# The first load of an attention-and-MLP kernel, q and k of one tile, cut into two transfers by heads

## The chip, the cores and the metric

The kernel runs on 1 core of one Trainium2 chip. The metric is device microseconds of one execution, as the median of several runs. The execution that the profiler recorded is one more run; its trace is what the rows below come from.

## The reference

Three stages follow one another. First, attention in chunks of 64 positions (4 batches, 8 heads, 576 positions, head size 64):

```
scores = scale * np.matmul(q_c, k_c.transpose(0, 1, 2, 4, 3))
scores = scores - np.max(scores, axis=-1, keepdims=True)
attn = np.exp(scores)
attn = attn / (np.sum(attn, axis=-1, keepdims=True) + 1e-09)
out = np.matmul(attn, v_c)
```

Its output, as 2304 tokens of 512 numbers, goes through an MLP with a SiLU (`h = x @ w_in`, `g = h * sigmoid(h)`, `g @ w_out`, 2048 wide) and then through a gated MLP (`(x @ w_a) * (x @ w_b) @ w_out`, 1536 wide).

## The kernel before

The 2304 tokens are 18 tiles of 128. The attention of tiles 0 to 3 comes first, all by itself; that of the other tiles is worked in between the matrix products of the first MLP. All of the order is written out by hand. A list of loads sets the order in which SP, which issues nearly all DMAs of this stage, issues them:

```
"s t 0, s t 1, s t 2, s w, s t 3, s v 1, s v 0, s w, s v 3, s w, s v 2, s w, s w"
```

Here `t i` is q and k of tile i together (512 KB, [128 partitions x 2 x 512] floats), `v i` is v of tile i (256 KB), and `w` one weight block of the first MLP (512 KB, raw 64-bit words). A second list, `beginning`, sets the order of everything else. Its first words are:

```
"busy 7 at, S 0 at mm, M 0 act, busy 2 acc2, E 0, S 1 sA sB, busy 1 acc2, N1 0, M 1, "
"S 2 acc0 acc1, E 1, busy 5 acc2, M 2 act, mg, N1 1, R 0, N2 0, busy 3 acc2, S 3 at mm, "
```

- `busy n` (line 757) are n matmuls on a tile of zeros, whose results nobody reads. Seven of them go into the bank `ps_at` ahead of `S 0`, which writes the same bank.
- `S i` (`att_scores`, line 295) are the 16 score products of tile i. The outer loop runs over the four head pairs `hp`, and each has four products: two chunks, and two heads of the pair (on partitions 0 to 63 and 64 to 127). Those of tile 0 go to the banks `ps_at` and `ps_mm`. In the trace every product has two records, so that `S 0` has 32.
- `M i` (line 311, and 313 or 316) takes the maxima on VectorE, `E i` (lines 332, 328) the exponentials on ScalarE, `T`, `P`, `V` (lines 369, 373, 394) transpose the probabilities, copy them back and multiply by v. `fa 0` (line 434) is the first product of the MLP.

Every DMA has its own completion count, out of eight that are used in turn (DMAHW0 to DMAHW7), so the ninth DMA of the program waits until the first has landed. `load_qk` (line 275) issues the transfer for tiles 0 to 3; on tiles 4 and later it takes the other branch.

Of the kernel before, what the change touches and what calls it, by code (L numbers as in the profile page):

```python
# [28 lines left out]
def chunk_attention_silu_mlp_gated_mlp(  # L29
# [35 lines left out]
    DM = out_t.shape[0]  # L65
# [29 lines left out]
    def width(b):  # L95
        return blocks[b][1] * P
# [162 lines left out]
    shared = {}  # L259

    def att_tile(where, name, i=0):
        if where == "att":
            return late["att"].tile([P, DM], F32, tag="at", name=name)
        key, n = (i, "qkvs".index(name)) if name in "qkvs" else (("pt", i // 4), i % 4)
        if key not in shared:
            shared[key] = slot("start", F32).rearrange("p (j n) -> p j n", j=4)
        return shared[key][:, n]

    def load_qk(i, where, eng=nc.gpsimd):
        qk[i] = [att_tile(where, nm, i) for nm in "qk"]  # L270
        if where == "att":
            for j, a in enumerate(qk[i]):
                eng.dma_start(out=a, in_=qkt[i][:, j])
        else:
            eng.dma_start(out=shared[i][:, :2], in_=qkt[i])

    def load_v(i, where, eng=nc.gpsimd):
        vs[i] = att_tile(where, "v", i)
# [455 lines left out]
    with tc.manual_schedule():  # L734
# [30 lines left out]
        n = width(SIDE)  # L765
# [9 lines left out]
        for line in loads.split(", "):  # L775
            by, what, *i = line.split()
            if what == "w":
                fetch(*next_a())
            elif what == "v":
                queues[by].dma_start(out=vs[int(i[0])], in_=v[int(i[0])])  # L780
            else:
                load_qk(int(i[0]), W, queues[by])
        load_qk(4, A, nc.sync)
        load_qk(5, A, nc.sync)

        SIDE_FROM = 6
# [898 lines left out]
```

## Time and profile before

| | us |
|---|---|
| median of 3 runs (lowest, highest) | 828.69 (828.15, 830.61) |
| profiled execution: its time | 829.36 |
| profiled execution: its span in the trace | 827.6 |
| PE busy, share of the span | 822.7, 99% |
| ACT busy, share of the span | 460.5, 56% |
| attention of tiles 0 to 3, until the first product of the MLP starts on PE | 0 to 19.77 |

The span is what the trace shows of the execution; 1.76 us of its time lie around it. PE is TensorE, PEld its weight loads, DVE VectorE, ACT ScalarE, POOL GpSimd, SP SyncE; SPq is the issuing of DMAs on SP. A busy PE also counts `busy` matmuls that compute nothing.

### The profile page before, as it was taken

To read this page: it belongs to the slowest core of one execution; us is meant where nothing else is said; L and a number is where in the kernel's file an instruction comes from. 1 tells how busy PE (TensorE), PEld (TensorE's weight loads), DVE (VectorE), ACT (ScalarE), POOL (GpSimd) and SP (SyncE) were. 2 spreads that over 40 slices of the span, in tenths; PEclk is the share of its full clock that TensorE was granted. 3 is DMA by queue.
4 is the path that set the end of the run, shared out by engine and by line. 5 is a ranking of instruction groups with operands and counts; after the bars stand their busy time and mean duration, and the time that the engine had idled before them with its cause. 6 is when DMAs were issued, how large, how long until landed. Compare 5 with 4: busy or idle time off the path is not lost.

```text
span 827.6 us, 14001 instructions
## 1 busy us (share of the span) xinstructions
PE 822.7 (99%) x5428; PEld 754.7 (91%) x5428; DVE 553.9 (67%) x1005; ACT 460.5 (56%) x868; POOL 50.7 (6%) x91
## 2 busy tenths in 40 slices
PE   9999999999999999999999999999999999999998
PEld 8889989888888888888889999999999999999998
DVE  6897576644667788788967995882545593454563
ACT  7997687765677755555744553453333363333252
POOL 1010010031021021100011100000000000000000
PEclk9999999999999999999999999999999999999999
DMA  9786698961375685720189769978677878767741
GB/s 354 260 277 191 196 277 277 271 201 53 108 262 170 221 319 227 288 97 27 65 298 401 293 279 367 331 286 287 246 247 264 326 276 304 267 238 251 282 181 58
DMA packets 52674, 199.10 MB, mean 241 GB/s; under 512 B 5632, under 2 KB 17536, under 8 KB 43136
## 3 DMA queue, kind: packets, MB, share of 16 engines
q1 hardware_dynamic: 43232, 162.78, 55.5%
q0 software_dynamic: 9088, 35.13, 12.1%
q8 instruction: 43, 0.70, 0.3%
q10 hardware_dynamic: 288, 0.30, 0.1%
q14 instruction: 23, 0.19, 0.1%
HBM read 147.32 MB, written 50.86 MB: 239 GB/s over the span
## 4 chain that ended last, share of the span: by engine, by line
PE 98%; DMA 2%; ACT 0%; issue 0%; SPq 0%
PE ps_acc L1006 26%; PE ps_acc L483 11%; PE ps_mm L434 8%; PE ps_sA L1006 8%; PE ps_mm L1006 8%; PE ps_sB L1006 7%; PE ps_at L1006 7%; PE ps_acc L434 5%; PE ps_at L434 4%; PE ps_sA L434 4%; PE ps_sB L434 2%; PE ps_sA L483 1%; PE ps_sB L483 1%; DMA ring<-wg 1%; PE ps_at L295 1%; PE ps_at L394 1%
## 5 line engine op out<-in xcount | busy, mean ns | idle before, releaser
L1006 PE MATMUL ps_acc<-xo,ring 128*128 128x384 f32 x902 | 171.9, 334 | 0.0
L1006 PEld LDWEIGHTS ps_acc<-xo,ring 128*128 128x128 f32 x902 | 157.7, 188 | 0.4 <-DVE gq L1081 0.3
L483 PE MATMUL ps_acc<-ghi,wA 128*128 128x512 f32 x256 | 81.1, 398 | 0.0
L1006 PE MATMUL ps_acc<-u,ring 128*128 128x384 f32 x322 | 61.3, 334 | 0.0
L1454 ACT ACTIVATE u<-gq 128x384 fp32r<-128x384 f32 x84 | 40.6, 516 | 30.9 <-DVE gq L1081 28.5
L1006 PEld LDWEIGHTS ps_acc<-u,ring 128*128 128x128 f32 x322 | 56.3, 188 | 0.0
L434 PE MATMUL ps_mm<-xhi,wA 128*128 128x512 f32 (+1 forms) x208 | 54.7, 386 | 0.0
L483 PEld LDWEIGHTS ps_acc<-ghi,wA 128*128 128x128 f32 x256 | 46.1, 188 | 9.4 <-ACT ghi L465 0.2
L1455 DVE TENSOR_TENSOR u<-gq,u 128x384 fp32r<-128x384 f32 x84 | 44.4, 552 | 15.2 <-ACT u L1454 15.0
L483 PE MATMUL ps_acc<-glo,wA 128*128 128x512 f32 x128 | 50.1, 392 | 0.0
L189 ACT ACTIVATE raws<-raws 128x512 f32<-128x512 f32 x62 | 41.7, 673 | 8.2 <-DVE raws L176 8.0
L463 DVE TENSOR_TENSOR glo<-g,ghi 128x512 fp32r<-128x512 f32 (+1 forms) x48 | 28.5, 600 | 25.1 <-ACT ghi L465 24.9
L1015 ACT ACTIVATE gq<-ps_acc 128x384 f32<-128x384 f32 x31 | 15.3, 492 | 52.9 <-PE ps_acc L1006 48.8
L1006 PE MATMUL ps_sA<-xo,ring 128*128 128x384 f32 x220 | 44.4, 334 | 0.0
L1006 PE MATMUL ps_mm<-xo,ring 128*128 128x384 f32 x214 | 43.2, 334 | 0.0
L206 DVE SCALAR_TENSOR_TENSOR w<-raws 128x512 uint32<-128x512 uint32 x42 | 29.0, 691 | 21.1 <-ACT raws L189 13.9
L434 PEld LDWEIGHTS ps_mm<-xhi,wA 128*128 128x128 f32 x208 | 37.0, 188 | 6.6
L1006 PE MATMUL ps_sB<-xo,ring 128*128 128x384 f32 x208 | 42.3, 335 | 0.0
L187 ACT ACTIVATE raws<-raws 128x512 int32<-128x512 uint8 x62 | 42.1, 679 | 0.0
L1006 PE MATMUL ps_at<-xo,ring 128*128 128x384 f32 x202 | 41.1, 335 | 0.3 <-DMA ring<-wg 0.3
L1006 PEld LDWEIGHTS ps_sA<-xo,ring 128*128 128x128 f32 x220 | 38.7, 188 | 0.0
L1006 PEld LDWEIGHTS ps_mm<-xo,ring 128*128 128x128 f32 x214 | 37.7, 188 | 0.0
(270 smaller groups left out, 1734.6 us busy)
## 6 DMA issues: line engine op xcount, KB each, us to landing
ring<-w SPq DMA_DIRECT2D x30, 1024.0 KB, 6.9
ring<-wg SPq DMA_DIRECT2D x28, 1024.0 KB, 7.3
ring<-wg SPq DMA_DIRECT2D x28, 768.0 KB, 4.6
wg<-ring SPq DMA_DIRECT2D x8, 1024.0 KB, 4.2
raws<-w_out SPq DMA_DIRECT2D x14, 512.0 KB, 5.2
raws<-w_in SPq DMA_DIRECT2D x12, 512.0 KB, 5.2
raws<-w_a SPq DMA_DIRECT2D x12, 512.0 KB, 4.7
raws<-w_b SPq DMA_DIRECT2D x12, 512.0 KB, 4.2
```

What stands on the lines that cost most here:

```text
L187: nc.scalar.activation(low.bitcast(I32), top, AF.Copy, scale=2.0**-5, bias=-31 / 64)
L189: nc.scalar.activation(high, high, AF.Prelu, scale=2.0**-112, alpha=-(2.0**32))
L206: nc.vector.scalar_tensor_tensor(out=out.bitcast(U32), in0=high[:, n], scalar=3, in1=low[:, n], op0=ALU.logical_shift_left, op1=ALU.bitwis ...
L295: nc.tensor.matmul(soft[i][0][j][n, hp, :], lhsT=q[r, hp, n], rhs=k[r, hp, n], start=True, stop=True,)
L394: nc.tensor.matmul(ps[half[part], hp, n], lhsT=va[half[r], a, hp, :], rhs=prob[i][half[r], hp, half[a]], start=True, stop=True,)
L434: nc.tensor.matmul(ps[:, n], lhsT=a[:, kk * P:(kk + 1) * P], rhs=b[:, kk, n], start=(j == 0 and kk == 0 and not part), stop=(j == 2 and kk ...
L463: nc.vector.tensor_tensor(out=glo, in0=g, in1=ghi.bitcast(F32), op=ALU.subtract)
L483: nc.tensor.matmul(acc_t[b][j], lhsT=a[:, j * P:(j + 1) * P], rhs=g, start=(m == 0 and i == 0 and (b != SIDE or j % 2 == 0)), stop=(m == M ...
L1006: nc.tensor.matmul(ps, lhsT=a, rhs=b, start=first and i == 0, stop=last and i == 2, skip_group_check=True,)
L1015: nc.scalar.activation(dst, ps, AF.Copy)
L1454: nc.scalar.activation(hi, src, AF.Copy)
L1455: nc.vector.tensor_tensor(out=lo, in0=src, in1=hi.bitcast(F32), op=ALU.subtract)
```

## The change

`load_qk` issues tile 0 as two transfers of 256 KB. The first holds columns 0 to 255 of q and of k (head pairs 0 and 1), the second columns 256 to 511 (head pairs 2 and 3). Tiles 1 to 3 keep their one transfer.

```
         else:
-            eng.dma_start(out=shared[i][:, :2], in_=qkt[i])
+            parts = 2 if i == 0 else 1
+            for n in range(parts):
+                c = slice(n * DM // parts, (n + 1) * DM // parts)
+                eng.dma_start(out=shared[i][:, :2, c], in_=qkt[i][:, :, c])
```

Whole, a partition's row of q and k is 4 KB in one piece; a half is two pieces of 1 KB each. The code below the edit moves down by three lines (295 becomes 298).

On SP, at the start of the program, before (`start` is the tile that holds q, k and v; `first` is the place of the raw weights; the brackets tell which DMA's completion an issue waits for):

```order
L275 DMA start<-qkt 128x1024 x3
L155 DMA first<-w_in 128x512
L275 DMA start<-qkt 128x1024
L780 DMA start<-v 128x512 x2
L155 DMA first<-w_in 128x512
L780 DMA start<-v 128x512 [waits DMAHW0_49]
L155 DMA first<-w_out 128x512 [waits DMAHW1_49]
```

On SP, the same place in the changed kernel:

```order
L278 DMA start<-qkt 128x2x256 x2
L278 DMA start<-qkt 128x1024 x2
L155 DMA first<-w_in 128x512
L278 DMA start<-qkt 128x1024
L783 DMA start<-v 128x512 x2
L155 DMA first<-w_in 128x512 [waits DMAHW0_49]
L783 DMA start<-v 128x512 [waits DMAHW1_49]
L155 DMA first<-w_out 128x512 [waits DMAHW2_49]
```

There is one DMA more, and every later one stands one place further down. The second weight block is now the ninth DMA and waits for the first half of tile 0; v of tile 3 waits for the second half where it waited for the whole; from there on each DMA waits for the same transfer as before, under the next number.

On PE, at the start of the program, before (the seven `busy` matmuls and the score products of tile 0, one row each):

```order
L757 MATMUL ps_at<-start 128x128 x6
L295 MATMUL ps_at<-start 64x64 [waits DMAHW0_49,PE_49]
L295 MATMUL ps_mm<-start 64x64
L295 MATMUL ps_at<-start 64x64
L295 MATMUL ps_mm<-start 64x64
L295 MATMUL ps_at<-start 64x64
L295 MATMUL ps_mm<-start 64x64
L295 MATMUL ps_at<-start 64x64
L295 MATMUL ps_mm<-start 64x64
L295 MATMUL ps_at<-start 64x64
L295 MATMUL ps_mm<-start 64x64
```

On PE, the same place in the changed kernel:

```order
L760 MATMUL ps_at<-start 128x128 x6
L298 MATMUL ps_at<-start 64x64 [waits DMAHW0_49,PE_49]
L298 MATMUL ps_mm<-start 64x64
L298 MATMUL ps_at<-start 64x64
L298 MATMUL ps_mm<-start 64x64
L298 MATMUL ps_at<-start 64x64
L298 MATMUL ps_mm<-start 64x64
L298 MATMUL ps_at<-start 64x64
L298 MATMUL ps_mm<-start 64x64
L298 MATMUL ps_at<-start 64x64 [waits DMAHW1_49]
L298 MATMUL ps_mm<-start 64x64
```

No product has moved. The first still waits for the first transfer and for PE's own `busy` matmuls; the ninth of the sixteen has a wait of its own, for the second transfer. On VectorE, ScalarE and GpSimd the order is the same in both kernels.

## Rows read from the trace of the kernel before

**Rows 1.** The page: span, and shares of the chain that ended last
```profile
span 827.6 us, 14001 instructions
...
PE 98%; DMA 2%; ACT 0%; issue 0%; SPq 0%
```

**Rows 2.** Windows; columns: stretch, length, busy time by engine, PEclk, DMA share, GB/s
```profile
0.00:4.63 4.63, 3.36 (x15) 3.10 (x15) 0.22 (x2) 1.49 (x2) 0.69 (x6) 1.00 0.61 192
4.63:19.77 15.14, 15.06 (x311) 13.28 (x311) 12.94 (x32) 12.74 (x47) 2.65 (x6) 1.00 1.03 402
```

**Rows 3.** The chain in order of time, start of the program: start, length, what
```profile
0.72 3.77 DMA start<-qkt
4.49 0.14 issue
4.63 0.34 PE ps_at L295
```

**Rows 4.** Timeline of PE: start, length, engine, line, tiles, count, [idle before]
```profile
1.07 3.36 PE L757 MATMUL ps_at<-start 128*128 128x128 f32 x14 [1.07 <-DVE start L751]
4.63 0.34 PE L295 MATMUL ps_at<-start 64*64 64x64 f32 x1 [0.20 <-DMA start<-qkt]
...
5.08 0.31 PE L295 MATMUL ps_at<-start 64*64 64x64 f32 x1
...
5.44 0.31 PE L295 MATMUL ps_mm<-start 64*64 64x64 f32 x1
5.68 1.22 PE L757 MATMUL ps_acc<-start 128*128 128x128 f32 x4
6.83 0.29 PE L295 MATMUL ps_sA<-start 64*64 64x64 f32 x1
...
8.52 2.37 PE L757 MATMUL ps_acc<-start 128*128 128x128 f32 x16
...
11.30 0.22 PE L295 MATMUL ps_mm<-start 64*64 64x64 f32 x1
...
14.40 1.15 PE L394 MATMUL ps_sA<-start 64*64 64x64 f32 x32
```

**Rows 5.** Who waited for whom, 0 to 70 us: total, times, longest
```profile
PEld ps_at L295 <- PE ps_at L757: 0.5, 1, 0.5
...
PE ps_at L295 <- DMA start<-qkt: 0.2, 1, 0.2
```

**Rows 6.** DMA traffic in the windows 3 to 4 and 412 to 414.5 us
```profile
DMA packets 113, 0.41 MB, mean 410 GB/s; under 512 B 13, under 2 KB 13, under 8 KB 113
...
DMA packets 924, 0.86 MB, mean 343 GB/s; under 512 B 51, under 2 KB 924, under 8 KB 924
```

**Rows 7.** Issues on SP, ns min/median/max; last line: landing of the yr loads, us
```profile
L275 SPq DMA_DIRECT2D start<-qkt x4: 388/422/477, 0.7 to 2.6; - x4
...
L162 SPq DMA_DIRECT2D wo<-w x8: 372/428/508, 20.7 to 59.5; - x8
...
L663 SPq DMA_DIRECT2D yr<-y x6: 545/602/608, 409.7 to 413.0; - x6
...
DMA to landing us min/median/max: 3.8/4.0/4.6
```

**Rows 8.** Timeline of SP: DMA issues that waited for tiles 1 and 2 and the weights
```profile
5.76 0.33 SPq L155 DMA_DIRECT2D first<-w_out  x1
7.04 0.33 SPq L780 DMA_DIRECT2D start<-v  x1
8.33 0.33 SPq L155 DMA_DIRECT2D first<-w_in  x1
```

**Rows 9.** Timelines of VectorE and ScalarE behind the first scores
```profile
5.80 0.43 DVE L311 TENSOR_REDUCE mx<-ps_at 128x4 f32<-128x256 f32 x1 [4.78 <-PE ps_mm L295]
...
9.60 0.43 DVE L176 TENSOR_SCALAR first<-first 128x512 f32<-128x512 f32 x1
...
12.57 0.41 DVE L316 TENSOR_TENSOR start<-ps_mm,mx 128x256 f32<-128x256 f32 x1
...
6.86 0.31 ACT L332 ACTIVATE start<-ps_at,mx 128x64 f32<-128x64 f32 x1 [4.64 <-DVE mx L313]
...
13.67 0.67 ACT L373 ACTIVATE start<-ps_acc 128x512 f32<-128x512 f32 x1
```

## The prediction

> **What bounds the kernel now.** I began with the chain of work that ended last. It is 98% PE, and DMA has 2% of it [rows 1], so a change of a load can only pay where PE waits for that load. The windows then part the program: in the 4.63 us before the first scores PE is busy for 3.36 us, and from there to the first product of the MLP, at 19.77, for 15.06 of 15.14 us [rows 2]. Behind that PE works without a gap worth naming, and what the first stage gains or loses the end gains or loses too, unless something takes it up on the way.
>
> The chain in order of time opens with the very transfer that is cut: issued at 0.72, landed at 4.49, 3.77 us later, then 0.14 us until the first score product at 4.63 [rows 3]. Read alone, that looks like 3.77 us of waiting for half of which an earlier half could be had. The timeline of PE says otherwise. From 1.07 to 4.43 PE runs `busy` matmuls, 14 records in 3.36 us, and they write the bank that the first score product writes; its idle time before the product is 0.20 us, not 3.77 [rows 4]. The first product waits for both, and the list of waits names both: 0.2 us for the DMA on the matmul, and 0.5 us for the `busy` matmuls on its weight load [rows 5]. So however early the first half lands, the product can't go before 4.43. **At most 0.20 us of 829 are there to be had.** That is the first reading that the reader should make here: of a load at the head of a chain, only the part that stands behind the other thing waited for can be won.
>
> **What the change removes.** The wait of the first eight products (16 records) for the second 256 KB. From the row of the `busy` matmuls to the products behind a wait on PE itself I allow 0.05 us, so they start at 4.43 + 0.05 = 4.48 in place of 4.63: 0.15 us earlier. Bounds: nothing, if the 0.5 us on the weight load is the wait that ended last; 0.20, if the products follow at 4.43.
>
> **What it adds on the transfer.** A partition's 4 KB become pieces of 1 KB. Early loads in whole rows move at 410 GB/s; the late loads of y (`yr`, pieces of 0.5 to 1.5 KB), all in packets under 2 KB, at 343 GB/s [rows 6]. The 0.524 MB of tile 0 so take 1.53 us of pure moving in place of 1.28, 0.25 us more, and the second half lands at about 4.49 + 0.25 = 4.74. The first lands 0.262 MB / 343 GB/s = 0.76 us ahead of it, at 3.98, well before 4.43: the `busy` matmuls cover it, and it could be 0.45 us later for nothing.
>
> When is the second half wanted? The 17th record of tile 0's 32 starts at 5.08, 0.45 us after the first [rows 4]. With a start at 4.48 that is 4.93, and with the 0.14 us from landing to product the half must have landed by 4.79; 4.74 makes it, barely. The point at which gain turns to loss is a landing at 5.08 - 0.14 = 4.94. Bounds on the landing: below, 4.49, if short pieces cost nothing; above, the longest of the y loads in pieces, 4.6 us after its issue. The second half is issued behind the first, whose issue takes between 0.43 us (stores in pieces) and 0.60 us (loads in pieces) against 0.42 for a whole [rows 7], so at 0.72 + 0.60 = 1.32 at the latest, and lands by 5.92 at the worst. I take 4.74, since the transfer runs with the same empty queue as before and only the shape of its pieces differs.
>
> **What it adds on SP.** One issue of 0.43 to 0.60 us, and 0 to 0.18 us more on the first one. All later loads are issued 0.4 to 0.8 us later. That they are bound by bytes and not by issue is seen in what waits for them: SP's issues at 5.76, 7.04 and 8.33 each wait for one 512 KB transfer, and stand 1.28 us apart, which is 0.524 MB at 410 GB/s [rows 8]. They will come by the 0.25 us later that tile 0's short pieces take. Tile 1 (landed at 5.76) is wanted at 6.83 [rows 4], the first weights (8.33) at 9.60 [rows 9]: 1.07 and 1.27 us of cover, so nothing shows. The new wait on SP, of the second weight block for the first half (landed at 3.98 plus), comes when SP has got there by itself, at 4.5 or so; behind it in the queue stand v of tile 3 and later weights, which waited already.
>
> **Where the 0.15 us go.** Scores of tile 0 end on PE at 5.75; VectorE takes the maxima from 5.80, having stood idle for them, ScalarE starts the exponentials at 6.86, having waited for VectorE [rows 9], and is then busy almost without a gap up to the copy of the first probabilities at 13.67, behind which the first product with v starts at 14.40 [rows 4, 9]. That path moves by the whole 0.15. The other one, PE's own, moves by less: up to 6.83 four `busy` records took 1.22 us, or 0.31 each, and from 8.52 on sixteen took 2.37, or 0.15 each [rows 4], though the granted clock is given as 1.00 for both [rows 2]. If PE's pace changes at a set moment, 0.15 us won at the slow pace are 0.15 x 0.15 / 0.31 = 0.07 us of the fast one. The maxima of tiles 1 to 3 hang on that path (those of tile 3 end with the step at 12.57, and the fourth exponential needs them). So 0.07 to 0.15 us arrive at 14.40; I take 0.1.
>
> **The sum.** The profiled execution took 829.36 us, of which 827.6 are span [rows 1]. 829.36 - 0.1 = 829.26. It lies 0.67 above the median of the runs shown, and the median moves with it: 828.69 - 0.1 = **828.6**. That is 0.01%, far inside 0.3% (2.5 us), about what a measurement of this kernel can tell from no change: its three runs already lie 2.46 us apart.
>
> **Rivals.**
>
> *Nothing happens at all.* The `busy` matmuls, not the DMA, released the first product. For it speaks the 0.5 us on the weight load [rows 5]; against it the 0.20 us that the matmul itself puts down to the DMA. Time 828.7.
>
> *The second half comes late.* It lands after 4.94 and the ninth product waits, with maxima and exponentials behind it. At the worst landing, 5.92, that is 5.92 - 4.94 = 0.98 us, time 829.7. For it speaks that the margin is 0.05 to 0.20 us and that a transfer in pieces has taken up to 4.6 us here; against it that those y loads queued behind each other. The Trainium skill speaks for this one, in "DMA: Bandwidth & Descriptors", Rules for kernel authors: many small transfers should be made one large one, and cutting a transfer in two gives nothing, because the parts run on the same engines one behind the other. By that rule the halves cost an issue and win nothing; an estimate by it is the second half one issue late, 4.49 + 0.60 = 5.09, a loss of 0.15 us in place of the gain of 0.1. No row here shows a cut load at an empty queue.
>
> *The slow pace of PE lasts longer.* This is the one that ends on the slower side. The place is the ninth product: if PE stands there for the second half, its busy stretch from 1.07 on is broken a second time, and the change of pace between 6.83 and 8.52 could come later. From 6.83 to the end of tile 3's scores at 11.52 [rows 4] PE does 4.7 us of work at the fast pace, all on the path to the maxima; at half pace it takes up to 4.7 us more, time 833.3. It decides, against 0.3%, from a pace that stays slow for some 2.5 of these 4.7 us, until about 11 us. For it: the margin of 0.05 us. Against it: PE already stood idle for 0.20 us at 4.43 and the pace still rose, and the gap that I expect is smaller. The Trainium skill, "TensorE: Matmul & The Clock Gate", Part 1, says that the clock is let up by sustained activity and taken back by idleness; this trace agrees as far as matmuls of one shape go from 0.31 to 0.15 us apart, while the column of the granted clock doesn't show it.
>
> **How the numbers follow.** A gain of 0.05 to 0.2: 0.55. Nothing: 0.2. The second half late by up to 0.98 us: 0.18. The slow pace for longer: 0.05, of which 0.03 pass 2.5 us. That leaves 0.02 for a gain that I don't see. All but the last two are "same": faster 0.02, same 0.94, slower 0.04. The range is set less by these than by the runs themselves, which lie from 0.54 below to 1.92 above their median: from 828.6 - 1.1 (twice the lower distance) to 828.6 + 1.7 (the late half at its worst, and some of a slower run), 827.5 to 830.3.
>
> **What would show it.** In the changed profile: two issues of 256 KB on SP at 0.72 and about 1.2; the first product at 4.45 to 4.63, with the `busy` matmuls as its releaser; records 17 to 32 following without an idle, or with one put down to the second half; the first maximum at about 5.65 and the first exponential at about 6.7; tile 1's scores no later than before; the first product of the MLP at about 19.7. Wrong would be a first product later than 4.63, an idle of more than 0.2 us in the middle of tile 0's scores, or `busy` matmuls that still stand 0.3 us apart at 8.5 us.

## The result, and the profile after

The changed kernel took 833.75 us (median of 15 runs, 831.61 to 835.5), the kernel before 829.38 us beside it (15 runs, 827.97 to 832.07). The ratio is 1.0053, interval 1.0045 to 1.0061: **slower by 4.4 us, 0.53%**, where 828.6 had been forecast. The profiled execution of the changed kernel took 832.56 us with a span of 830.8, 3.2 us more than that of before [rows 1].

The chain of work that ended last, in order of time, start of the program (start, length, what), answers to [rows 3]:

```profile
0.73 0.65 SPq L278
1.38 0.06 issue
1.43 0.59 SPq L278
2.03 0.05 issue
2.08 6.87 DMA start<-qkt
8.94 0.04 issue
8.99 0.36 PE ps_sA L298
```

It no longer runs through tile 0's load. The two halves are now only two issues on SP (0.65 and 0.59 us), and the transfer on the chain is the third: q and k of tile 1, an uncut 512 KB, issued at 2.08 and landed 6.87 us later. In the kernel before, the whole load at the head took 3.77 us [rows 3].

The timeline of PE after the change (start, length, engine, line, tiles, count, [idle before]) answers to [rows 4]:

```profile
1.07 3.36 PE L760 MATMUL ps_at<-start 128*128 128x128 f32 x14 [1.07 <-DVE start L754]
4.49 0.37 PE L298 MATMUL ps_at<-start 64*64 64x64 f32 x1
...
5.62 0.36 PE L298 MATMUL ps_at<-start 64*64 64x64 f32 x1 [0.42 <-DMA start<-qkt]
...
6.25 1.22 PE L760 MATMUL ps_acc<-start 128*128 128x128 f32 x4
8.99 0.36 PE L298 MATMUL ps_sA<-start 64*64 64x64 f32 x1 [1.51 <-DMA start<-qkt]
...
10.05 0.79 PE L760 MATMUL ps_acc<-start 128*128 128x128 f32 x2
10.77 1.13 PE L298 MATMUL ps_acc<-start 64*64 64x64 f32 x32
11.84 2.80 PE L760 MATMUL ps_acc<-start 128*128 128x128 f32 x16
...
23.51 0.74 PE L437 MATMUL ps_mm<-xhi,wA 128*128 128x256 f32 x4
```

Three things are to be seen, in this order. The first product starts at 4.49 in place of 4.63, behind the `busy` matmuls: the gain is there. The ninth product (17th record) waits 0.42 us for the second half and starts at 5.62 where 4.93 had been expected. Then PE stands for 1.51 us before tile 1's scores, which start at 8.99 in place of 6.83, and behind that it works more slowly: the same 16 `busy` records take 2.80 us in place of 2.37. The first product of the MLP comes 23.51 - 19.77 = 3.74 us later. Of these, 8.99 - 6.83 = 2.16 us are tile 1's late start; the other 1.58 arise behind it, since from tile 1's first score to the MLP it is now 14.52 us in place of 12.94.

The timeline of SP after the change; the last three issues each wait for a transfer, as those of [rows 8] do:

```profile
0.73 2.42 SPq L278 DMA_DIRECT2D start<-qkt  x4
...
3.66 0.61 SPq L278 DMA_DIRECT2D start<-qkt  x1
...
8.96 0.33 SPq L155 DMA_DIRECT2D first<-w_out  x1
10.25 0.33 SPq L783 DMA_DIRECT2D start<-v  x1
11.55 0.33 SPq L155 DMA_DIRECT2D first<-w_in  x1
```

Tile 1, tile 2 and the first weights landed at 8.96, 10.25 and 11.55, against 5.76, 7.04 and 8.33 before: each 3.2 us later. Among themselves they stand 1.29 and 1.30 us apart, as before. So the whole delay arises between tile 0 and tile 1; behind it bytes are the bound again. The windows (stretch, length, busy time of PE, PEld, DVE, ACT, POOL, granted clock, DMA share, GB/s) show the place, after:

```profile
4.00:5.50 1.50, 1.14 (x19) 0.65 (x17) 0.00 (x0) 0.00 (x0) 0.00 (x0) 1.00 0.91 87
5.50:7.00 1.50, 1.38 (x19) 1.27 (x20) 0.63 (x2) 0.00 (x0) 0.00 (x0) 1.00 0.66 229
7.00:8.50 1.50, 0.47 (x3) 0.17 (x1) 0.30 (x2) 1.07 (x7) 0.00 (x0) 1.00 0.92 369
```

and before:

```profile
4.00:5.50 1.50, 1.30 (x34) 1.03 (x33) 0.00 (x0) 0.00 (x0) 0.00 (x0) 1.00 1.01 393
5.50:7.00 1.50, 1.50 (x23) 1.16 (x20) 0.93 (x3) 0.14 (x1) 0.00 (x0) 1.00 1.03 412
```

From 4.0 to 5.5 us the DMA engines count as busy for 0.91 of the time and move 87 GB/s, where before they moved 393. The share counts engines as busy that move next to nothing; it alone would have hidden this. The DMA view of these 1.5 us (queue: packets, MB, share of 16 engines), after:

```profile
q1 hardware_dynamic: 68, 0.13, 90.9%
```

and before:

```profile
q1 hardware_dynamic: 163, 0.59, 101.2%
```

Few packets fill nearly the same time. In the trace's list of packets, 14 packets of 4 KB that started between 3.8 and 6.1 us took 1.2 to 2.1 us each, where the median packet of 4 KB takes 0.159 us in both kernels; before, none that started between 3 and 9 us took more than 0.39. They belong to the whole loads behind the cut, since tile 0's own packets are now of 1 KB. So the hold-up is engines that stand on single packets of the next load.

### The profile page after: what moved, and what is told of

It is laid out like the page before. It is cut to its first block, busy times and chain, and to the rows that moved or that the text cites. A ratio compares the mean times of both kernels' runs of the same rounds, so it can differ in the third digit from the quotient of the medians.

```text
span 830.8 us, 14002 instructions
## 1 busy us (share of the span) xinstructions
PE 824.0 (99%) x5428; PEld 756.1 (91%) x5428; DVE 554.3 (67%) x1005; ACT 461.1 (55%) x868; POOL 50.7 (6%) x91
## 4 chain that ended last, share of the span: by engine, by line
PE 98%; DMA 1%; DVE 0%; SPq 0%; ACT 0%; issue 0%
PE ps_acc L1009 27%; PE ps_acc L486 11%; PE ps_mm L437 8%; PE ps_sA L1009 8%; PE ps_mm L1009 8%; PE ps_sB L1009 7%; PE ps_at L1009 7%; PE ps_acc L437 5%; PE ps_at L437 4%; PE ps_sA L437 4%; PE ps_sB L437 2%; PE ps_sB L486 1%; PE ps_sA L486 1%; PE ps_at L298 1%; DMA start<-qkt 1%; PE ps_at L397 1%
```

## The experiments

Three things were asked: what holds up the transfers behind the cut (the number of transfers, the 1 KB pieces, the place in SP's queue); whether that hold-up is what makes the kernel slower; and what PE's pace adds. My theory of the loss was that tile 1's late landing makes it; the rivals were that the slower 1 KB pieces make it, or that PE's pace does; which property of the cut delays tile 1 was asked in turn, as one answer after the other fell. The expectations name the theories as they stood at the time. "Landing" below is the start of the SP issues that wait for tile 1, tile 2 and the first weights. One table holds those readings (us, one profiled execution each), the experiments follow in the order in which they ran. The ratios with their intervals are those of the record; they are not the quotients of the two medians given with each experiment (in experiment 4 that quotient is 1.0033).

| kernel | landing: tile 1 / tile 2 / weights | tile 1's scores start | first product of the MLP | ratio to before, 95% interval |
|---|---|---|---|---|
| before | 5.76 / 7.04 / 8.33 | 6.83 | 19.77 | |
| after | 8.96 / 10.25 / 11.55 | 8.99 | 23.51 | 1.0053, 1.0045 to 1.0061 |
| 1 rows | 6.69 / 8.14 / 9.53 | 7.70 | 21.68 | 1.0032, 1.0017 to 1.0046 |
| 2 pieces | 6.25 / 7.54 / 8.82 | 7.30 | 23.03 | 1.0018, 1.0004 to 1.0031 |
| 3 q, k | 7.75 / 9.04 / 10.34 | 7.78 | 22.51 | 1.0038, 1.0022 to 1.0054 |
| 4 `busy` | 8.12 / 9.39 / 10.69 | 8.15 | 21.29 | 1.0044, 1.0027 to 1.0061 |
| 5 idle | 5.82 / 7.11 / 8.38 | 6.92 | 20.33 | 1.0014, 1.0005 to 1.0022 |
| 6 late | 5.82 / 7.11 / 8.43 | 5.92 | 19.38 | 1.0006, 0.9996 to 1.0016 |
| 7 tiny | 7.49 / 8.78 / 10.07 | 7.51 | 22.23 | 1.0014, 1.0005 to 1.0023 |
| 8 whole | 7.43 / 8.71 / 10.01 | 7.46 | 21.84 | 1.0028, 1.0013 to 1.0043 |
| 9 third | 5.73 / 7.07 / 8.40 | 5.83 | 19.30 | 1.0007, 0.9996 to 1.0017 |
| 10 ScalarE | 6.49 / 7.77 / 9.05 | 6.51 | 19.89 | 1.0007, 0.9996 to 1.0017 |
| 11 two | 7.36 / 9.03 / 10.29 | 7.38 | 20.96 | 1.0022, 1.0013 to 1.0031 |
| 12 v second | 6.67 / 8.36 / 9.62 | 6.70 | 20.29 | 1.0013, 0.9998 to 1.0028 |
| 13 tile 1 cut | 6.92 / 8.43 / 9.69 | 6.62 | 20.36 | 1.0010, 0.9997 to 1.0023 |
| 14 behind 1 | 5.87 / 8.34 / 9.61 | 6.38 | 20.24 | 1.0012, 1.0002 to 1.0022 |
| 15 tile 2 cut | 5.75 / 8.00 / 9.28 | 6.22 | 19.74 | 1.0023, 1.0004 to 1.0041 |

(In 13 the first number is the landing of tile 1's second half, and the scores of its first heads start ahead of it; in 15 the second number is tile 2's second half.)

**1. Cut by partitions.** The changed kernel, with halves of 64 partitions in whole rows of 4 KB.

```
c = slice(n * P // parts, (n + 1) * P // parts)
eng.dma_start(out=shared[i][c, :2], in_=qkt[i][c])
```

> Tile 0 is cut by partitions: two transfers of 64 rows, each row 4 KB in one piece, so there is one transfer more but no short piece. Theory P (the short pieces are what holds up the transfers behind them): the stall of tile 1 is gone, tile 1 lands at about 5.8 us as in the kernel before, and the time is that of before, 829.4 plus or minus 1. Theory C (one more transfer at the start is what holds them up): tile 1 lands at 8 to 9 us and the time stays at 833 to 834.

831.99 us (5 runs) against 829.5. The hold-up is mostly gone (tile 1 at 6.69, 0.93 late), but the kernel is still 0.32% slower: halves of 64 partitions were themselves slow to land, and tile 0's scores waited 0.54 us for the second, until 5.50. It changes two things at once and so tells the theories apart poorly.

**2. Pieces of 1 KB without a cut.** The kernel before; tile 0 comes in one transfer from a copy of the input with a gap behind every 256 columns, so that it moves in pieces of 1 KB.

```
eng.dma_start(out=shared[i][:, :2].rearrange("p j (h c) -> p (j h) c", h=2), in_=qk0[:, :, :256])
```

> Tile 0 is one transfer again, but its source has a gap behind each 1 KB, so that it moves in 512 pieces of 1 KB: all of the short pieces, none of the cut. Theory P: tile 1 lands at 8 us or later, and the time is 832 to 834. Theory C: tile 0 lands at about 4.7, tile 1 at about 6, and the time is 829.4 plus or minus 1.

Everything lands 0.49 us later and no more: tile 1 at 6.25, which is a transfer bound by bytes in slower pieces. So the pieces alone don't make the 3.2 us. The kernel lost 1.9 us all the same (831.42, 10 runs, against 829.5). Waiting explains little of it: PE stands 0.46 us longer than before for tile 0, and tile 1's scores wait for no DMA. The timeline of PE of this kernel:

```profile
5.09 0.33 PE L301 MATMUL ps_at<-start 64*64 64x64 f32 x1 [0.66 <-DMA start<-qk]
...
9.09 1.13 PE L301 MATMUL ps_acc<-start 64*64 64x64 f32 x32
10.15 4.01 PE L763 MATMUL ps_acc<-start 128*128 128x128 f32 x16
```

The 16 `busy` records take 4.01 us here and 2.37 in [rows 4]. The MLP comes 3.26 us later than before, of which 7.30 - 6.83 = 0.47 are the later scores; the rest is pace.

**3. Cut into q and k.** The changed kernel, halves of 2 KB in one piece; every score needs both.

```
c = slice(n * 2 // parts, (n + 1) * 2 // parts)
eng.dma_start(out=shared[i][:, c], in_=qkt[i][:, c])
```

> Tile 0 is cut into q and k: two transfers, pieces of 2 KB, 256 pieces in all instead of 512. The first product waits for both. Theory P, with the stall growing with the number of pieces: something between, 830 to 832, tile 1 landing at 6 to 8 us. Theory C: 833 to 834 as with the cut by heads.

832.59 us (9 runs) against 829.5; tile 1 at 7.75, 2.0 us late. A cut in long pieces holds up too, by less than one in pieces of 1 KB.

**4. More work for PE in the gap.** The changed kernel, ten `busy` records in place of four before tile 1's scores.

```
-"M 0 act, busy 2 acc2, E 0"
+"M 0 act, busy 5 acc2, E 0"
```

> The changed kernel with five instead of two busy matmuls between the scores of tile 0 and of tile 1, to fill the 1.5 us in which PE stands idle for tile 1. Theory S (the idle costs twice: 2.2 us of waiting, and about 1.6 us because PE's pace rises only at about 12 us instead of 7): the pace rises earlier, and the time falls to 831.5 to 832.5, with tile 1 still landing at about 9. Rival (only the late landing costs): 833.5 or, if the added matmuls outlast the wait, a little more.

832.23 us (4 runs, 831.32 to 834.53), an interval that overlaps that of the changed kernel: the time decides nothing. The trace shows PE at the fast pace all along, ten records in 1.38 us, and from tile 1's scores to the MLP 13.14 us, only 0.20 more than before; tile 1 was still late, at 8.12. But PE had that pace ahead of the added work: tile 0's first score products, at 4.5, already have records of 0.22 us (0.31 in [rows 4]), and it kept the pace over a standing of 1.11 us for tile 0's second half, until 6.05. So this run doesn't show that the added work brings the pace. The loads, the same as in the changed kernel, landed otherwise here, the second half later and tile 1 earlier: where there is a hold-up, its size in one execution is good to some 0.8 us.

```profile
6.44 1.38 PE L760 MATMUL ps_acc<-start 128*128 128x128 f32 x10
8.15 0.27 PE L298 MATMUL ps_sA<-start 64*64 64x64 f32 x1 [0.33 <-DMA start<-qkt]
```

**5. An idle PE alone.** The kernel before, its transfers untouched, with four `busy` records less ahead of the first scores.

```
-"busy 7 at, S 0 at mm"
+"busy 5 at, S 0 at mm"
```

> The kernel before, uncut, with five instead of seven busy matmuls ahead of the first scores: PE ends them at about 3.5 us and stands idle for about 1.1 us until tile 0 has landed at 4.5, with no transfer changed. Theory S (idle of PE in the first microseconds also delays the rise of its pace): the scores still start at 4.6, yet PE's records stay at the slow spacing for longer in more of the runs, and the median rises by 0.7 to 2.5 us. Rival (the pace does not hang on such gaps): the median of before, plus or minus 0.4.

830.31 us (11 runs) against 828.92: 1.4 us slower in the medians, 1.2 by the ratio, with the first product at 4.71 (before 4.63) and every landing in the table within 0.07 us. PE stands 1.13 us before that product, 0.93 more than before, and its records come down from 0.31 us only at about 8:

```profile
4.71 0.34 PE L295 MATMUL ps_at<-start 64*64 64x64 f32 x1 [1.13 <-DMA start<-qkt]
...
7.98 0.54 PE L757 MATMUL ps_acc<-start 128*128 128x128 f32 x2
```

A standing of 0.93 us more, which delays the first scores of tiles 0 and 1 by less than 0.1 us, costs 1.2 us, by pace alone.

**6. The same cut, late.** The changed kernel with tile 3 cut in place of tile 0 (2 MB stand ahead of it).

```
-parts = 2 if i == 0 else 1
+parts = 2 if i == 3 else 1
```

> Tile 3 is cut by heads into two transfers in pieces of 1 KB, tile 0 is whole: the same cut, but behind 2 MB of queued transfers. Theory D (a cut holds up what lies behind it only at the start, when nothing else is queued to keep the DMA engines at work): tile 0 to 2 land as before, tile 3 ends at 9.6 to 10, and the time is that of before, plus or minus 0.5 us. Rival (a cut in short pieces costs wherever it stands): the transfers behind tile 3 land 2 us later than before or more, and the time is 1 us above before or more.

829.63 us (11 runs) against 828.92, interval across 1. No hold-up: tile 3's second half and what stands behind it come 9.90 - 9.61 = 0.29 us later than in the kernel before. Here the prediction's term for short pieces, 0.25 us, holds.

**7. A small transfer behind tile 0.** The kernel before with a transfer of 16 KB more, which nothing reads, right behind tile 0.

```
+if i == 0:
+    eng.dma_start(out=att_tile("start", "pt", 4)[:16, :256], in_=qkt[i][:16, 0, :256])
```

> The kernel before, uncut, with a transfer of 16 KB (16 rows of 1 KB, read by nobody) issued between tiles 0 and 1: one issue more on SP, nearly no bytes. Theory I (what tile 1 loses is the issue that stands ahead of it): tile 1 lands about 1 us later than before, near 6.8, and the time rises by 0.5 to 2 us. Rival (the halves' own movement is what holds tile 1 up): tile 1 lands at about 5.8, time as before plus or minus 0.5.

830.67 us (11 runs) against 828.92. The 16 KB are 0.04 us at 410 GB/s, and tile 1 comes 1.73 us late. No cut, no short half of tile 0 is needed for a hold-up: one more transfer at that place does it. The timeline of SP of this kernel:

```profile
7.49 0.33 SPq L155 DMA_DIRECT2D first<-w_out  x1
8.78 0.33 SPq L782 DMA_DIRECT2D start<-v  x1
10.07 0.33 SPq L155 DMA_DIRECT2D first<-w_in  x1
```

Behind tile 1 the landings are 1.29 us apart again. And PE's pace is seen to fall here. Windows of this kernel, the granted clock being the third number from the end:

```profile
8.00:9.00 1.00, 0.82 (x26) 0.56 (x20) 0.74 (x3) 1.00 (x8) 0.00 (x0) 0.90 1.06 430
9.00:10.00 1.00, 1.00 (x33) 0.88 (x30) 0.68 (x4) 0.45 (x3) 0.23 (x1) 0.50 0.99 395
11.00:12.00 1.00, 1.00 (x7) 1.00 (x6) 0.97 (x4) 0.88 (x4) 0.41 (x2) 0.50 1.04 412
13.00:14.00 1.00, 1.00 (x37) 0.81 (x35) 0.00 (x0) 1.00 (x8) 0.00 (x0) 1.00 1.01 389
```

PE had come to the fast pace at 5.3 (four `busy` records in 0.71 us), stood 1.30 us for tile 1, and then ran from about 9 to 12 at half of its clock, 1.2 in place of 2.4 GHz.

**8. The cut by heads in whole pieces.** The changed kernel with tile 0's inputs laid out by halves, so that each half is 2 KB in one piece and the first products need the first half alone.

```
...
halves = shared[0][:, :2].rearrange("p g (j h n) -> p j g h n", j=2, h=2)
q, k = ([halves[:, j, hp // 2, hp % 2] for hp in range(KT)] for j in range(2))
...
```

> The change by heads with the inputs of tile 0 laid out by halves, so that each half is 2 KB in one piece per partition, and the first eight products wait for the first half alone. If the pieces of 1 KB make up most of the loss, tile 1 lands near 6.9 as with q and k cut apart, the products wait less, and the time is 830 to 831.5. If the cut itself makes up the loss, it stays at 832 to 834.

832.14 us (6 runs) against 828.92. Tile 0's scores don't wait at all now (its last `busy` block starts at 5.11, before at 5.68), and it is still slower by 0.28%: tile 1 comes at 7.43. The timeline of PE of this kernel:

```profile
5.11 0.71 PE L764 MATMUL ps_acc<-start 128*128 128x128 f32 x4
7.46 0.27 PE L302 MATMUL ps_sA<-start 64*64 64x64 f32 x1 [1.64 <-DMA start<-qkt]
...
8.34 0.79 PE L764 MATMUL ps_acc<-start 128*128 128x128 f32 x2
```

and its windows:

```profile
7.00:8.00 1.00, 0.54 (x28) 0.54 (x32) 0.00 (x0) 1.00 (x8) 0.00 (x0) 0.86 0.99 381
8.00:9.00 1.00, 1.00 (x18) 0.72 (x11) 0.55 (x2) 0.76 (x6) 0.15 (x1) 0.50 0.99 401
10.00:11.00 1.00, 1.00 (x12) 0.88 (x6) 0.75 (x3) 1.00 (x2) 0.00 (x0) 0.50 1.07 420
12.00:13.00 1.00, 0.97 (x10) 0.85 (x14) 0.85 (x3) 1.00 (x8) 0.23 (x1) 1.00 1.03 391
```

The same picture: fast at 5.11, 1.64 us of standing, and then half the clock. Its six runs speak too: five with a mean granted clock of 0.998 took 831.37 to 833.45 us, the one with 1.0 took 829.67.

**9. The small transfer behind tile 2.** The kernel before and the 16 KB of experiment 7, two places later (`if i == 2`).

> The uncut kernel with the 16 KB transfer behind tile 2 instead of behind tile 0. Theory N (each transfer more among the first ones costs what lies behind it about 1.2 us, whatever its bytes): tiles 0, 1 and 2 land as in the kernel before (4.5, 5.8, 7.0), the first weights at 9.5 instead of 8.3, just in time for their use at 9.6, so that the time is that of before plus 0 to 0.7 us. Rival (only a transfer between tile 0 and tile 1 does harm): the weights land at 8.3 to 8.6 too.

829.71 us (11 runs) against 829.11, interval across 1; all landings within 0.07 us of before. Theory N, that a transfer more costs a fixed price wherever it stands, has fallen.

**10. The second half from another queue.** The changed kernel, with the second half issued by ScalarE; the `warm` activation, which stood ahead on ScalarE, goes behind the loads.

```
+by = nc.scalar if n else eng
+by.dma_start(out=shared[i][:, :2, c], in_=qkt[i][:, :, c])
```

> The change by heads with the second half of tile 0 issued by ScalarE at the start (the exponential's table is loaded behind it), so that SP issues tile 1 as its second transfer, as in the kernel before. Theory Q (the loss comes from the row of issues on SP's queue): tile 1 lands at 5.8 to 6.2 and the time is 829 to 830.5. Theory N (what counts is the number of transfers, from whatever queue): tile 1 lands at 7.5 to 9 and the time is 832 to 834.

829.66 us (11 runs) against 829.11: ratio 1.0007, interval 0.9996 to 1.0017. The same cut in the same 1 KB pieces, and the interval shows no loss. The timeline of SP of this kernel:

```profile
6.49 0.33 SPq L155 DMA_DIRECT2D first<-w_out  x1
7.77 0.33 SPq L781 DMA_DIRECT2D start<-v  x1
9.05 0.33 SPq L155 DMA_DIRECT2D first<-w_in  x1
```

and its windows:

```profile
4.00:5.50 1.50, 0.66 (x25) 0.50 (x28) 0.00 (x0) 0.00 (x0) 0.00 (x0) 1.00 1.01 354
5.50:7.00 1.50, 1.46 (x59) 1.21 (x51) 0.93 (x3) 0.06 (x1) 0.00 (x0) 1.00 1.05 418
```

The engines move 354 GB/s where they moved 87 in the changed kernel, tile 1 lands 2.5 us earlier than there, 0.7 us later than before, and its scores (6.51) no longer wait. This is the run that ties the loss to the hold-up. There is no gain either: the first product came at 5.14, because the first half itself landed later. PE stood 0.84 us for it, but had come to the fast pace ahead of that, at about 3.9 us.

**11. Two small transfers behind tile 0.** Experiment 7 twice.

```
+for n in range(4, 6):
+    eng.dma_start(out=att_tile("start", "pt", n)[:16, :256], in_=qkt[i][:16, 0, :256])
```

> The uncut kernel with two transfers of 16 KB between tiles 0 and 1. Theory N: what lies behind comes 2.4 us late instead of 1.2, tile 2 at 9.4 or so, and the time is 832 to 833.5. Rival (a single disturbance, however many transfers make it): tile 1 and tile 2 land as with one, 6.4 and 8.2, and the time is 830 to 831.

830.79 us (11 runs) against 829.11. Tile 1 at 7.36, no later than with one; tile 2 is another 0.4 us late. The hold-up isn't proportional to the number of transfers.

**12. A whole transfer between.** The kernel before with v of tile 1 (256 KB, whole) moved to the second place of SP's list.

```
-"s t 0, s t 1, s t 2, s w, s t 3, s v 1, s v 0, ...
+"s t 0, s v 1, s t 1, s t 2, s w, s t 3, s v 0, ...
```

> The uncut kernel with v of tile 1 (256 KB, needed anyway) issued second, between tiles 0 and 1, in place of sixth: as many transfers as before, and tile 1 is third in the row as in the changed kernel. Theory L (a transfer whose turn on the DMA engines comes less than about 2.3 us after its issue began makes them stand still on its first packets; the half, like the 16 KB, is through too fast): v of tile 1 fills 0.64 us, tile 1's turn comes 2.5 us or more after its issue, nothing stalls, and tile 1 lands at 6.4 to 6.6. Rival (any transfer between tiles 0 and 1 does harm): tile 1 lands at 7 us or later. The time is above that of before in either case, by 0.5 to 1.5 us or by 1.5 to 3.

830.41 us (10 runs) against 829.36, interval from 0.9998. By bytes tile 1 would come 0.64 us later, at 6.4, and tile 2 at 7.7; they came at 6.67 and 8.36. A smaller hold-up, of 0.3 and 0.7 us, with a plain load; both are no larger than the difference between two executions of the same loads (after and 4).

**13. Tile 1 cut.** The changed kernel with `parts = 2 if i == 1 else 1`.

> Tile 1 instead of tile 0 is cut by heads into two transfers in pieces of 1 KB; tile 0 is whole and first. Theory L: tile 0's 512 KB give the halves and tile 2 their time, nothing stalls, tile 1 lands whole at about 6.0 and tile 2 at about 7.3; the time is that of before plus or minus 0.6. Rival (a cut near the head of the queue does harm whether or not a whole tile stands ahead): tile 2 lands at 8 us or later, and the time is 1 us above before or more.

829.83 us (10 runs) against 829.36, interval across 1. Tile 1's second half lands at 6.92, 1.2 us late, and tile 2 at 8.43, 1.4 late. So Theory L has fallen: it is not the time since the first issue that frees a transfer from the hold-up.

**14. The small transfer behind tile 1.** The kernel before and the 16 KB with `if i == 1`.

> The uncut kernel with the 16 KB transfer behind tile 1, third in the row (it did harm as second and none as fourth). Theory B (what lies behind is held up if less than two whole tiles, 1 MB, have been issued on SP's queue when the first packet moves, at about 1.7 us): both whole tiles are issued by 1.6, nothing stalls, tile 2 lands at 7.0 to 7.2 and the weights at 8.3 to 8.5; time that of before plus or minus 0.7. Rival (any small transfer among the first three does harm): tile 2 lands at 8 us or later.

829.97 us (9 runs) against 829.07: slower by 0.12%. Tile 1 comes at 5.87, tile 2 at 8.34, 1.3 us late. The hold-up moved with the small transfer; Theory B, that 1 MB issued ahead prevents it, has fallen.

**15. Tile 2 cut.** The changed kernel with `parts = 2 if i == 2 else 1`.

> Tile 2 is cut by heads into pieces of 1 KB; tiles 0 and 1 are whole and first (with tile 1 cut, tile 2 came at 8.4 instead of 7.0). Theory B: nothing stalls, the second half of tile 2 lands at 7.2 to 7.5 and the first weights at 8.5 to 8.8; time that of before plus or minus 0.7. Rival: tile 2 or the weights come 1 us or more later than in the kernel before (8 us, 9.3 us).

Tile 2's second half lands at 8.00; by bytes and short pieces it would be 7.04 + 0.25 = 7.3. A hold-up of 0.7 us, if it is one. The time, 831.13 us (5 runs, 829.52 to 833.24) against 829.07, doesn't measure it: in the profiled execution the MLP began at 19.74, no later than before. By the starts of the same instructions on VectorE, that execution was level with the kernel before up to 105 us, 1.9 us behind at 130 and 2.4 at 445. The timeline of PE shows it standing there, twice for `glo` from VectorE (a part of `g`, the first MLP's hidden values) and once for a weight block:

```profile
116.56 0.39 PE L486 MATMUL ps_sA<-glo,wA 128*128 128x256 f32 x1 [0.40 <-DVE glo L466]
130.55 0.39 PE L486 MATMUL ps_sA<-glo,wA 128*128 128x256 f32 x1 [1.10 <-DVE glo L466]
444.42 1.33 PE L1009 MATMUL ps_at<-xo,ring 128*128 128x384 f32 x6 [0.78 <-DMA ring<-wg]
```

In the kernel before only the last of the three shows, and shorter:

```profile
442.00 1.32 PE L1006 MATMUL ps_at<-xo,ring 128*128 128x384 f32 x6 [0.32 <-DMA ring<-wg]
```

Waits for `glo` of about that length stand in experiments 3, 4 and 12 too (1.06, 0.87 and 1.07 us). Why VectorE was late there no run tells.

## Why the prediction was wrong, step by step

**What there was to be had.** At most 0.20 us, and 0.15 expected: measured 4.63 - 4.49 = 0.14. The reading that the `busy` matmuls hold the first product until 4.43 was right.

**Tile 0's second half.** Forecast for 4.74; by the ninth product (5.62 less the 0.14 us from landing to product) it landed at 5.48. The rival "the second half comes late" had the mechanism, and its size, up to 0.98 us, held: tile 0's last score products end at 6.32 in place of 5.75, 0.57 us later. An idle of more than 0.2 us in the middle of these scores was one of the prediction's own signs of being wrong. The Trainium skill, "DMA: Bandwidth & Descriptors", Rules for kernel authors, says of two transfers to disjoint partition halves that they serialize and aren't worth the bother. Experiment 1, which is that cut, agrees (ratio 1.0032); for halves by columns the prediction carried the rule over, and the estimate made with it, 0.15 us of loss, was far short of what came.

**The step that failed is "What it adds on SP"**: "They will come by the 0.25 us later that tile 0's short pieces take", covered by 1.07 us. They came 3.2 us later, three times the cover. The term was taken from issues that stand 1.28 us apart [rows 8], which is true of the steady stream and also after the change, but was used for the first transfers, of which no row showed anything. The runs put in its place: the pieces of 1 KB cost 0.49 us (experiment 2) or 0.29 us late in the queue (6), near the 0.25 reckoned; an additional transfer directly behind tile 0 on SP's queue holds up tile 1 by 1.7 to 2.0 us, be it a half in pieces of 2 KB (3, 8) or 16 KB (7), and by 0.9 where it is a half of the partitions (1); the cut in 1 KB pieces makes 3.2, and 2.4 in another execution of the same loads (4). From the fourth transfer on nothing of it was seen (6, 9). Experiment 10 shows that this hold-up is what the kernel pays for: with the cut kept and the second half on ScalarE's queue, 0.7 of the 3.2 us are left, tile 1's scores don't wait for them, and no loss shows.

**The slow pace of PE.** This rival, at 0.05 and up to 833.3 us, described most nearly what happened: in the profiled execution the pace made 1.58 of the 3.74 us at the MLP's start. It looked for the standing at the ninth product (0.42 us of idle there); tile 1's scores, with 1.51, it did not name. Which of the two kept the pace down isn't shown. Read from PE's records, the fast pace came between 3.9 and 6.9 us in the twelve profiled executions in which PE had not stood for more than 0.25 us before it, and between 8 and 14 in the five (after, 1, 2, 3, 5) in which it had stood 0.42 to 1.13 us at tile 0's scores. Experiments 2 and 5 show pace with hardly a wait on the path, 7 and 8 show the clock fall to 0.50 behind a standing of 1.30 and 1.64 us. There the Trainium skill, "TensorE: Matmul & The Clock Gate", Part 1, that idleness takes the clock back, agrees with the trace. In experiments 4 and 11 the fast pace outlasted a standing of 1.11 and 1.41 us, so that a standing can cost pace but need not.

Over all executions the mean clock agrees with that: of 106 timed runs of the kernel before in the comparisons above none has a mean granted clock below 0.999, of the 15 of the changed kernel eight have 0.996 to 0.998, of experiment 10 none. The other seven of the changed kernel have 1.0 and are no faster (medians 833.59 and 833.79 us). In the profiled one, which is among them, the column stays at 1.00 although records of the slow pace are there until 12.6 us: as in [rows 2], where it gives 1.00 beside records of 0.31 us, the column shows a clock that falls and not one that hasn't risen yet. Of the other six no trace is kept.

How the 4.4 us of the medians divide between the wait and the pace can't be said better than by that one execution. Pace scatters from run to run: with the same start, experiments 6 and 9 were fast by 4.7 us and the kernel before at 6.9. The prediction's sentence that the end gains or loses what the first stage does holds up to 105 us: there, all sixteen changed kernels are as far behind or ahead as at the MLP's start, to 0.04 us. Behind that come the two places of experiment 15, which in single executions took off 0.4 or put on up to 1.9 us (at 110 to 135) and took off or put on 0.6 (at about 445), so that +3.74 at the MLP had become +3.2 at the end. The start of the MLP is thus the better measure of a load here than the time of one execution.

**What stays open** is why the first packets behind such a transfer take some ten times as long as others. Number of transfers (11), time since the first issue (13) and bytes issued ahead (14, 15) each failed to order all the runs; the place, second or third on SP's queue, is all that they have in common. No kernel of these beat the one before.

## What to carry to other kernels

The gain of an earlier first load ends at the next thing that its reader waits for, and its price is not paid there: look at when the transfers *behind* the cut land. Spacing in the steady stream says nothing of the first two or three transfers of a program; a change among those wants a run, and an additional one is best tried on another engine's queue or behind the third load. A standing PE early in a program can cost a slow stretch on top of its own length, so a load that is only just covered is worth more margin than its wait alone suggests.

## What the runs showed of the hardware that was not expected

- A transfer of 16 KB, 0.04 us of moving at 410 GB/s, delayed all that stood behind it by 1.7 us in the second place of the queue, delayed tile 2 by 1.3 us in the third, and cost nothing in the fourth (experiments 7, 14, 9).
- The DMA share read 0.91 while 87 GB/s were moved, because single packets of 4 KB took 1.2 to 2.1 us in place of 0.159; the GB/s column, not the share, shows a hold-up.
- SP's issue of a half, two pieces of 1 KB in each of 128 partitions, took 0.65 and 0.59 us, against a median of 0.42 for the whole load [rows 7].
- TensorE's clock, once at the upper level, went back to 0.50 behind 1.3 to 1.6 us of standing, from about 9 to 12 us in experiment 7 and from 8 to 11 in experiment 8; with 1.41 us of standing in experiment 11 and 1.11 in experiment 4 the profiled executions showed no such fall.
